# Moving one broadcast, respacing the fillers, and laying out two weight matrices anew in a fused attention and feed-forward kernel

## The chip, the cores and the metric

One core of a Trainium2 chip runs the kernel. Its engines are TensorE (PE; its weight loads are listed as PEld), VectorE (DVE), ScalarE (ACT), GpSimd (POOL) and SyncE (SP); SP and POOL also issue the DMA transfers, and a `q` behind an engine's name (SPq) marks its issuing side. The metric is the time of one execution on the device in microseconds (us), median of several runs. Lower is better.

## The reference

Sliding-window attention with a linear bias, and behind it a feed-forward block with layer norm, on 8 sequences of 576 tokens, 8 heads of 64, `d_model` 512, hidden size 2048. All inputs and the output are fp32.

```python
scores = q @ k.T / 8 - slope[h] * abs(i - j)      # only 0 <= i - j < 128
x  = softmax(scores) @ v                          # heads side by side: 512 columns
xn = (x - mean(x)) / sqrt(var(x) + 1e-6) * g_ln
out = x + relu(xn @ w_ch1) @ w_ch2                # 512 -> 2048 -> 512
```

## The kernel before

The 4608 tokens are cut into 36 blocks of 128. A block goes through attention, and blocks are then joined to ten chunks (`CHUNKS`, of 3, 2, 3 and then 4 blocks) for the feed-forward part, whose matmuls thus have 384, 256, 384 and then 512 columns.

*Attention of block i.* q and k come in on SP (`load`, L360; `load_span` for two blocks at a time, L455) or, from block 9 on, on POOL with a cast on the way (L469). Loaded fp32 is cast to fp16 on POOL, ACT or DVE (L617 for spans, L556 for block 4, L589 for v). PE turns q and k so that the head's dimension lies on the partitions: fp32 pairs against an identity for spans (L635, tasks `T0.0`, `T0.1`, ...; "the turn"), fp16 for block 4 (L682). ACT or DVE evicts the turn to `qkt` (L645, L643). For the first five blocks PE puts the bias into PSUM with a matmul (L736, `Z`); the scores go on top (L720, `S`). ACT takes the exponential (L768, `probs`), PE multiplies with v (L792, 65 columns, one of them the row's sum), and DVE divides (L809, L813), takes mean and variance (L830, L835) and writes `xs = (x - mean) * g` (L841). PE turns `xs` (L853, later by DMA), which gives `xt`. Tables for the mask and bias of later blocks (`mreg`, `mmix`, `mnew`) are made once on ACT (L433) and DVE (L441 and following).

*g.* `g_ln` is one row of 512. Task `G` (L411) broadcasts it to all partitions: an fp32 matmul of a row of ones with the row, 512 columns into a bank of PSUM, and `Gc` (L418) copies it to `g_t`, which the first `xs` reads.

*Feed-forward of chunk c.* `A{c}.{f}` (L902), for each of 16 groups f of 128 hidden columns: four matmuls, with 128 columns of W1 as the loaded weight and `xt` as the moving operand; a relu on ACT (L914) or DVE (L912) to `ht`. `B{i}` (L930), for each block of the chunk: 16 matmuls with `ht` as the loaded weight and rows of W2 moving. DVE multiplies by 1/std and adds x (L938), and SP writes the block out (L946). The last block is done in two halves of 256 columns (`cuts`).

*Weights.* W1 and W2 come in four transfers each on POOL's queue, with a cast to fp16 (`weights`, L532 and L534). They are issued behind the casts or loads listed in `W_AFTER`: the first of W1 behind block 2, the second and third behind block 3, the fourth behind block 6. A transfer of W1 brings 512 of the 2048 hidden columns, so the fourth is first read by group f = 12. A transfer of W2 brings 512 rows, on partition p the rows 512m + p, 512m + 128 + p, and so on.

*What sets the order.* `Plan` is a list scheduler that runs while the kernel is built. Every task has an engine, a cost in us, a due value `v` and what it depends on; transfers are tasks of a queue, with a cost of their own. The planner goes through simulated time, gives a free engine the ready task with the lowest `v`, and hands out four PSUM banks (`fb`) for all results but the scores. The order that comes out is emitted as the program. Each engine then runs its list strictly in order and waits on semaphores. A cost or dependency that changes can thus move tasks anywhere later in the lists.

*Fillers.* While the planned time is below 24 us (`WARM`), `keep_warm` (L966 to L968) puts small matmuls of zeros into PE's list wherever the plan has PE idle, one for each 0.11 us of gap if the gap starts before 6 us, and one for each 0.06 us later. They always run, whether PE would have waited or not.

Of the kernel before, what the change touches and what calls it, by code (L numbers as in the profile page):

```python
# [226 lines left out]
def kernel(  # L227
# [75 lines left out]
    mreg = sb("mreg", [P, 4, 2, 2 * P], FP16)  # L303
    mmix = sb("mmix", [P, 4, 2, 2 * P], FP16)
    mnew = sb("mnew", [P, 4, 2, 2 * P], FP16)
    w1sb = sb("w1sb", [P, NKB, ffn], FP16)
    w2sb = sb("w2sb", [P, NFB, d_model], FP16)

    q32 = ring("q32", 2, [P, H, D], FP32)
    k32 = ring("k32", 2, [P, H, D], FP32)  # L310
# [30 lines left out]
        return (i / CB - LEAD) * SPAN + stage  # L341

    w1r = moe_w_ch1.rearrange("(kb p) f -> p kb f", p=P)
    w2r = moe_w_ch2.rearrange("(fb p) d -> p fb d", p=P)

    def where(i):

# [69 lines left out]
        else:  # L417
            nc.scalar.activation(out=g_t[:, :], in_=src, func=AF.Copy)  # L418

    t_g = add("G", ("PE", 1.3), e_g, [d_row], av(0, 4.0), acq=("fb", "G"))  # L420
    d_g = add("Gc", {"ACT": 0.6, "DVE": 0.69}, e_gc, [t_g], av(0, 4.5), rel="G")

    t_sid = []
# [100 lines left out]
    def weights(i, casts):  # L524

        for n, at in enumerate(W_AFTER):
            if at // 3 != i:
                continue

            def emit(e, b, m=n % 4, n=n):  # L530
                if n < 4:
                    nc.gpsimd.dma_start(out=w1sb[:, :, 512 * m : 512 * m + 512], in_=w1r[:, :, 512 * m : 512 * m + 512])  # L532
                else:
                    nc.gpsimd.dma_start(out=w2sb[:, 4 * m : 4 * m + 4, :], in_=w2r[:, 4 * m : 4 * m + 4, :])  # L534
            last = [t_w[n - 1][0]] if n else []
            t_w[n] = plan.transfer(f"w{n}", "POOL", 0.8, 3.2, 0.0, emit, [casts[at % 3]] + last, av(i, -60.0))

    span_done, pv_done, qkt_part = {}, {}, {}
    qkt_done, vx_done, aggr_done, xs_done, xt_done = {}, {}, {}, {}, {}

    def attention(i):
# [62 lines left out]
        if i in span_of:  # L604
            n = span_of[i]
            if SPANS[n] == i:
                evs, casts = [[], []], {}
                for (a, x), (landed, h0, h1) in span_load[n].items():
                    r_, w_ = ((qs, qs16), (ks, ks16))[a]

                    def e_c(e, b, r_=r_, w_=w_, n=n, h0=h0, h1=h1):
                        dst = w_[n][:, h0:h1, :, :].rearrange("p h d t -> p t h d")
                        src = r_[n][:, h0:h1, :].rearrange("p h (t d) -> p t h d", t=2)
                        if e == "ACT":
                            nc.scalar.activation(out=dst, in_=src, func=AF.Copy)
                        else:
                            (nc.vector if e == "DVE" else nc.gpsimd).tensor_copy(out=dst, in_=src)  # L617
                    f = (h1 - h0) / H
                    cs = add(
                        f"cT{i}.{a}{x}", pick(f"cs{a}{x}", "POOL", POOL=0.12 + 1.26 * f, ACT=0.22 + 1.18 * f, DVE=0.1 + 0.7 * f),  # L620
                        e_c, [landed], av(i, 0.1 * a + 0.2 * x),
                    )
                    r_.reads(n, cs); w_.writes(n, cs)
                    for y in range(2) if f == 1 else (x,):
                        casts[a, y] = cs
                for x in range(2):
                    key = f"T{i}.{x}"

                    def e_t(e, b, x=x, n=n):
                        for a, w_ in ((0, qs16), (1, ks16)):  # L630
                            for hp in range(2):
                                h0 = 4 * x + 2 * hp
                                pair = w_[n][:, h0 : h0 + 2, :, :].rearrange("p h d t -> p (h d t)").bitcast(FP32)
                                c0 = (2 * a + hp) * P
                                nc.tensor.transpose(fb[b][:, c0 : c0 + P], pair, iden32[:, :])  # L635
                    tt = add(key, ("PE", 0.45), e_t, [casts[0, x], casts[1, x], d_iden32], av(i, 1.0 + 0.1 * x), acq=("fb", key))
                    qs16.reads(n, tt); ks16.reads(n, tt)
                    for blk in range(2):
                        def e_ev(e, b, x=x, blk=blk, key=key):
                            src = fb[plan.held[key][1]][:, :].bitcast(FP16).rearrange("p (a hp c) -> p a hp c", a=2, hp=2)[:, :, :, P * blk : P * blk + P]  # L640
                            dst = qkt[i + blk][:, :, 2 * x : 2 * x + 2, :]
                            if e == "DVE":
                                nc.vector.tensor_copy(out=dst, in_=src)  # L643
                            else:
                                nc.scalar.activation(out=dst, in_=src, func=AF.Copy)  # L645
                        ev = add(f"e{key}{blk}", pick(f"ev{x}{blk}", "DVE ACT", DVE=0.42, ACT=0.6), e_ev, [tt] + evs[0][len(evs[1]) :], av(i + blk, 1.2 + 0.1 * x), rel=key)
                        qkt.writes(i + blk, ev)
                        evs[blk].append(ev)
                span_done[n] = evs
# [240 lines left out]
    def mlp(c):  # L890
# [5 lines left out]
        for f in range(NFB):  # L896
            key = f"A{c}.{f}"
            vm = v0 + f * per

            def e_a(e, b, f=f):  # L900
                for kb in range(NKB):
                    nc.tensor.matmul(  # L902
                        fb[b][:, 0:n_], w1sb[:, kb, f * P : f * P + P], xt[c][:, kb, 0:n_],
                        start=(kb == 0), stop=(kb == NKB - 1),
                    )
            a = add(key, ("PE", 0.216 * nb), e_a, done + [t_w[f // 4][1]], vm, acq=("fb", key))
            xt.reads(c, a)

            def e_r(e, b, f=f, key=key):
                src = fb[plan.held[key][1]][:, 0:n_]  # L910
                if e == "DVE":
                    nc.vector.tensor_scalar(out=ht[c][:, f, 0:n_], in0=src, scalar1=0.0, scalar2=None, op0=ALU.max)  # L912
                else:
                    nc.scalar.activation(out=ht[c][:, f, 0:n_], in_=src, func=AF.Relu)  # L914
            r_ = add(f"r{c}.{f}", {"ACT": 0.17 + 0.107 * nb, "DVE": 0.16 + 0.133 * nb}, e_r, [a], vm - 4.0, rel=key)
            ht.writes(c, r_)
            relu.append(r_)
        for j in range(nb):
            i = FIRST[c] + j
            cuts = (0, d_model // 2, d_model) if i == NBLK - 1 else (0, d_model)  # L920
            for c0, c1 in zip(cuts, cuts[1:]):
                key = f"B{i}" if c1 - c0 == d_model else f"B{i}.c{c0}"
                last = None
                for f0 in range(0, NFB, 4):
                    vm = v0 + 16 * per + (4 * j + f0 / 4 + c0 / 100) * SPAN / 32

                    def e_b(e, b, j=j, f0=f0, key=key, c0=c0, c1=c1):
                        pm = fb[plan.held[key][1]]
                        for f in range(f0, f0 + 4):
                            nc.tensor.matmul(  # L930
                                pm[:, 0 : c1 - c0], ht[c][:, f, j * P : j * P + P], w2sb[:, f, c0:c1],
                                start=(f == 0), stop=(f == NFB - 1),
                            )
                    last = add(f"{key}.{f0}", ("PE", 0.864 * (c1 - c0) / d_model), e_b, relu[f0 : f0 + 4] + [t_w[4 + f0 // 4][1], last], vm, acq=("fb", key))
                    ht.reads(c, last)

                def e_o(e, b, i=i, j=j, key=key, c0=c0, c1=c1):
                    nc.vector.scalar_tensor_tensor(  # L938
                        out=ot[i][:, c0:c1], in0=fb[plan.held[key][1]][:, 0 : c1 - c0], scalar=rstd[c][:, j : j + 1],
                        in1=xb[i][:, c0:c1], op0=ALU.mult, op1=ALU.add,  # L940
                    )
                o = add(f"o{i}.{c0}", ("DVE", 0.2 + 0.55 * (c1 - c0) / d_model), e_o, [last, kept[c]], vm - 4.0, rel=key)
                ot.writes(i, o); rstd.reads(c, o); xb.reads(i, o)

                def e_d(e, b, i=i, c0=c0, c1=c1):
                    nc.sync.dma_start(out=out_flat[i * P : i * P + P, c0:c1], in_=ot[i][:, c0:c1])  # L946
                t, d = plan.transfer(f"out{i}.{c0}", "SP", 0.42, 0.8 * (c1 - c0) / d_model, 0.12, e_d, [o], vm - 4.0)
                ot.reads(i, d)
# [8 lines left out]
    for n, (at, tasks) in enumerate(cast_seq):  # L957
        before = [t_w[m][0] for m, w_at in enumerate(W_AFTER) if (w_at // 3 * 3 + 2 if w_at // 3 in span_of else w_at) < at][-1:] + (cast_seq[n - 1][1] if n and at < 27 else [])
        for t in tasks:
            t.deps += before  # L960
    for c in range(len(CHUNKS)):
        mlp(c)

    order = plan.run()

    def keep_warm(a, b):  # L966
        for _ in range(int((b - a - 0.06) / (0.11 if a < 6.0 else 0.06))):
            nc.tensor.matmul(fb[3][:, 0:P], warm_t[:, :], warm_t[:, :], start=True, stop=True)  # L968

    with tc.manual_schedule():  # L970
# [38 lines left out]
```

## Time and profile before

| | us |
|---|---|
| median of 6 runs | 320.22 (319.5 to 322.06) |
| the profiled execution | 319.98 |
| its span in the profile | 318.3 |
| PE busy | 311.5 |
| PE idle for all its waits | 3.5 |
| 592 matmuls of L930, share of the chain that ended last | 40% |
| 640 matmuls of L902, share of that chain | 38% |

Times in the profile count from the start of the span. A matmul's record is longer than its place in the queue, as matmuls overlap: one with 512 columns has a record of 379 ns, but the next starts 215 ns later. So the pace is read from start to start. The rows on loads in the timeline name the engine that issues; when a transfer lands is told by the times to landing. "<-" behind a row's idle time names what ended it.

### The profile page before, as it was taken

What the parts mean: (1) busy time and instruction counts of PE and PEld (TensorE: products, weight loads), DVE (VectorE), ACT (ScalarE), POOL (GpSimd) and SP (SyncE); (2) the same over time, 40 slices, a digit from 0 to 9 for tenths busy, and PEclk for the clock granted to TensorE, in tenths of its full rate; (3) what the DMA queues carried; (4) which work ended last, traced back from release to release, by engine and by line L of the source; (5) the groups of instructions that cost most, each with busy time, mean ns of one, the idle gap of its engine ahead of it and who ended that gap; (6) DMA issues with size and microseconds to landing.
All of it is one profiled execution on the core that took longest, in us unless ns stands there. A gap on an engine that the chain in (4) does not pass through costs nothing.

```text
span 318.3 us, 6348 instructions
## 1 busy us (share of the span) xinstructions
PE 311.5 (98%) x2540; PEld 168.3 (53%) x2540; DVE 183.9 (58%) x410; ACT 158.1 (50%) x258; POOL 101.9 (32%) x133
## 2 busy tenths in 40 slices
PE   8989999999999999999999999999999999999995
PEld 6766766545555444454444544444445444444444
DVE  2689469852789676566666666466666666011012
ACT  2587784226666861475247524752474247305600
POOL 6636685685256274543633312011000000000000
PEclk9999999999999999999999999999999999999999
DMA  8999999999999999999999999456400220011012
GB/s 196 234 185 244 208 203 175 155 193 194 144 151 182 159 154 150 191 174 155 198 176 102 102 161 165 39 67 130 119 16 19 83 85 16 16 68 66 0 60 74
DMA packets 155408, 41.45 MB, mean 130 GB/s; under 512 B 138353, under 2 KB 150897, under 8 KB 155378
## 3 DMA queue, kind: packets, MB, share of 16 engines
q0 software_dynamic: 92768, 15.34, 65.2%
q1 hardware_dynamic: 62608, 25.70, 41.7%
q8 instruction: 20, 0.33, 0.4%
q14 instruction: 10, 0.08, 0.1%
q10 hardware_dynamic: 2, 0.00, 0.0%
HBM read 36.70 MB, written 9.44 MB: 145 GB/s over the span
## 4 chain that ended last, share of the span: by engine, by line
PE 89%; SPq 4%; DMA 2%; DVE 2%; ACT 1%; issue 0%; POOL 0%; DVEq 0%
PE fb L930 40%; PE fb L902 38%; PE sc L720 5%; PE fb L792 5%; SPq L360 3%; DMA k<-in_k_dram 2%; SPq L455 2%; PE fb L853 1%; PE fb L635 0%; DVE mnew L441 0%; PE fb L968 0%; DVE xb L813 0%; ACT probs L768 0%; PE sc L736 0%; ACT ht L914 0%
## 5 line engine op out<-in xcount | busy, mean ns | idle before, releaser
L930 PE MATMUL fb<-w2sb,ht 128*128 128x512 f16 (+1 forms) x592 | 135.0, 373 | 0.0
L902 PE MATMUL fb<-xt,w1sb 128*128 128x512 f16 (+2 forms) x640 | 132.7, 358 | 0.4 <-ACT probs L768 0.4
L914 ACT ACTIVATE ht<-fb 128x512 f16<-128x512 f32 (+2 forms) x144 | 79.3, 556 | 68.4 <-PE fb L902 67.4
L768 ACT ACTIVATE probs<-sc 128x1024 f16<-128x1024 f32 (+1 forms) x72 | 67.7, 973 | 59.8 <-PE sc L720 59.5
L902 PEld LDWEIGHTS <-w1sb 128*128 128x128 f16 x640 | 59.8, 98 | 57.0 <-DMA w1sb<-in_moe_w_ch_dram 0.6
L930 PEld LDWEIGHTS <-ht 128*128 128x128 f16 x592 | 54.2, 98 | 55.0
L938 DVE SCALAR_TENSOR_TENSOR ot<-fb,rstd,xb 128x512 f32<-128x512 f32 (+1 forms) x37 | 27.2, 735 | 56.2 <-PE fb L930 55.5
L469 POOL DMA_DIRECT2D vx<-in_v_dram x34 | 28.9, 853 | 63.6 <-PE fb L792 58.1
L775 DVE TENSOR_TENSOR probs<-probs,mreg 128x1024 f16<-128x1024 f16 (+1 forms) x48 | 30.7, 651 | 20.3 <-ACT probs L768 20.0
L469 POOL DMA_DIRECT2D qk<-in_q_dram x30 | 25.3, 845 | 23.3 <-DMA qkt<-qk 12.5
L792 PEld LDWEIGHTS <-probs 128*128 128x128 f16 x544 | 24.8, 98 | 14.1 <-ACT probs L768 0.6
L813 DVE TENSOR_TENSOR xb<-fb,rec 128x256 f16<-128x256 f32 x72 | 30.2, 423 | 2.1
L469 POOL DMA_DIRECT2D qk<-in_k_dram x30 | 25.3, 844 | 14.7 <-DMA vx<-in_v_dram 5.1
L841 DVE SCALAR_TENSOR_TENSOR xs<-xb,mv,g_t 128x512 f16<-128x512 f16 x36 | 27.7, 768 | 0.9
L792 PE MATMUL fb<-vx,probs 128*128 128x65 f16 x544 | 27.8, 193 | 0.0
L830 DVE BATCH_NORM_STATS2 st<-xb 128x6 f32<-128x512 f16 x36 | 24.8, 692 | 1.0
L809 DVE RECIPROCAL rec<-fb 128x4 f32<-128x4 f32 x72 | 12.6, 177 | 19.3 <-PE fb L792 19.1
L720 PEld LDWEIGHTS <-qkt 64*128 64x128 f16 x544 | 15.3, 94 | 11.8 <-issue 10.6
L720 PE MATMUL sc<-qkt 64*128 64x128 f16 x288 | 19.8, 216 | 0.0
L720 PE MATMUL sc<-qkt,qkt 64*128 64x128 f16 x256 | 18.4, 219 | 0.0
L912 DVE TENSOR_SCALAR ht<-fb 128x512 f16<-128x512 f32 (+2 forms) x16 | 9.9, 616 | 10.6 <-PE fb L902 9.3
L968 PE MATMUL fb<-warm_t 128*128 128x128 f16 x90 | 9.3, 258 | 1.1 <-DVE warm_t L372 1.1
(59 smaller groups left out, 111.6 us busy)
## 6 DMA issues: line engine op xcount, KB each, us to landing
out_dram<-ot SPq DMA_DIRECT2D x35, 256.0 KB, 3.7
vx<-in_v_dram POOLq DMA_DIRECT2D x28, 128.0 KB, 9.5
qk<-in_q_dram POOLq DMA_DIRECT2D x24, 128.0 KB, 10.9
qk<-in_k_dram POOLq DMA_DIRECT2D x24, 128.0 KB, 11.0
w1sb<-in_moe_w_ch_dram POOLq DMA_DIRECT2D x4, 512.0 KB, 9.2
w2sb<-in_moe_w_ch_dram POOLq DMA_DIRECT2D x4, 512.0 KB, 11.7
qs<-in_q_dram SPq DMA_DIRECT2D x4, 256.0 KB, 4.4
ks<-in_k_dram SPq DMA_DIRECT2D x4, 256.0 KB, 4.7
```

Source lines behind the costliest of these rows:

```text
L469: nc.gpsimd.dma_start(out=dst(p0, n), in_=src[b, :, s0 : s0 + n, :].rearrange("h p d -> p h d"))
L720: nc.tensor.matmul(scs[half][:, g, c0 : c0 + P], kt[rows, 1, hp, :], qkt[i][rows, 0, hp, :], start=not bias, stop=True, skip_group_check=True,
L768: nc.scalar.activation(out=o, in_=n_, func=AF.Exp, scale=inv_sqrt_d)
L775: en.tensor_tensor(out=pv, in0=pv, in1=mask[:, 2 * half : 2 * half + 2, :, lo:], op=ALU.mult)
L792: nc.tensor.matmul(pp[:, hh * (D + 1) : hh * (D + 1) + D + 1], probs[i][:, bank, slot, side * P : side * P + P], vx[i - 1 + side][:, h, 0 ...
L813: nc.vector.tensor_tensor(out=xb[i][:, 256 * half : 256 * half + 256].rearrange("p (h d) -> p h d", d=D), in0=pp[:, :, 0:D], in1=rec[2 * i ...
L830: nc.vector.bn_stats(out=st[i][:, :], in_=xb[i][:, :])
L841: nc.vector.scalar_tensor_tensor(out=xs[i][:, :], in0=xb[i][:, :], scalar=mv[c][:, j, 0:1], in1=g_t[:, :], op0=ALU.subtract, op1=ALU.mult,)
L902: nc.tensor.matmul(fb[b][:, 0:n_], w1sb[:, kb, f * P : f * P + P], xt[c][:, kb, 0:n_], start=(kb == 0), stop=(kb == NKB - 1),)
L914: nc.scalar.activation(out=ht[c][:, f, 0:n_], in_=src, func=AF.Relu)
L930: nc.tensor.matmul(pm[:, 0 : c1 - c0], ht[c][:, f, j * P : j * P + P], w2sb[:, f, c0:c1], start=(f == 0), stop=(f == NFB - 1),)
L938: nc.vector.scalar_tensor_tensor(out=ot[i][:, c0:c1], in0=fb[plan.held[key][1]][:, 0 : c1 - c0], scalar=rstd[c][:, j : j + 1], in1=xb[i][: ...
```

## The change

Five edits. Task `G` gets half its planned cost and a dependency on the first turn (`first_turn`), so that it stands behind it. Fillers count by 0.11 us up to a planned time of 8.5 us instead of 6. W1 becomes four tiles, one for a transfer, and W2 as well. A transfer of W2 now brings, on partition p, the four rows 512m + 4p to 512m + 4p + 3, which lie side by side in HBM (8 KB); for the rows to fit, the weight of group f = 4m + j is every fourth column of W1's tile m, from column j on (`w1f`). W2's planned transfer is 2.7 us instead of 3.2. The last block is cut into 384 and 128 columns.

```diff
@@ -303,8 +303,8 @@
-    w1sb = sb("w1sb", [P, NKB, ffn], FP16)
-    w2sb = sb("w2sb", [P, NFB, d_model], FP16)
+    w1sb = [sb(f"w1sb{m}", [P, NKB, CH], FP16) for m in range(CB)]
+    w2sb = [sb(f"w2sb{m}", [P, CB, d_model], FP16) for m in range(CB)]
@@ -341,7 +341,8 @@
-    w2r = moe_w_ch2.rearrange("(fb p) d -> p fb d", p=P)
+    w2r = moe_w_ch2.rearrange("(m p j) d -> p m (j d)", p=P, j=CB)
+    w1f = [t[:, :, :].rearrange("p kb (c j) -> p kb j c", j=CB) for t in w1sb]
@@ -417,7 +418,7 @@
-    t_g = add("G", ("PE", 1.3), e_g, [d_row], av(0, 4.0), acq=("fb", "G"))
+    t_g = add("G", ("PE", 0.65), e_g, [d_row], av(0, 4.0), acq=("fb", "G"))
@@ -529,13 +530,13 @@
                 if n < 4:
-                    nc.gpsimd.dma_start(out=w1sb[:, :, 512 * m : 512 * m + 512], in_=w1r[:, :, 512 * m : 512 * m + 512])
+                    nc.gpsimd.dma_start(out=w1sb[m][:, :, :], in_=w1r[:, :, 512 * m : 512 * m + 512])
                 else:
-                    nc.gpsimd.dma_start(out=w2sb[:, 4 * m : 4 * m + 4, :], in_=w2r[:, 4 * m : 4 * m + 4, :])
+                    nc.gpsimd.dma_start(out=w2sb[m][:, :, :].rearrange("p j d -> p (j d)"), in_=w2r[:, m, :])
             last = [t_w[n - 1][0]] if n else []
-            t_w[n] = plan.transfer(f"w{n}", "POOL", 0.8, 3.2, 0.0, emit, [casts[at % 3]] + last, av(i, -60.0))
+            t_w[n] = plan.transfer(f"w{n}", "POOL", 0.8, 3.2 if n < 4 else 2.7, 0.0, emit, [casts[at % 3]] + last, av(i, -60.0))
-    span_done, pv_done, qkt_part = {}, {}, {}
+    span_done, pv_done, qkt_part, first_turn = {}, {}, {}, []
@@ -634,6 +635,7 @@
                     tt = add(key, ("PE", 0.45), e_t, [casts[0, x], casts[1, x], d_iden32], av(i, 1.0 + 0.1 * x), acq=("fb", key))
+                    first_turn.append(tt)
@@ -900,7 +902,7 @@
-                        fb[b][:, 0:n_], w1sb[:, kb, f * P : f * P + P], xt[c][:, kb, 0:n_],
+                        fb[b][:, 0:n_], w1f[f // CB][:, kb, f % CB, :], xt[c][:, kb, 0:n_],
@@ -917,7 +919,7 @@
-            cuts = (0, d_model // 2, d_model) if i == NBLK - 1 else (0, d_model)
+            cuts = (0, 3 * P, d_model) if i == NBLK - 1 else (0, d_model)
@@ -928,7 +930,7 @@
-                                pm[:, 0 : c1 - c0], ht[c][:, f, j * P : j * P + P], w2sb[:, f, c0:c1],
+                                pm[:, 0 : c1 - c0], ht[c][:, f, j * P : j * P + P], w2sb[f // CB][:, f % CB, c0:c1],
@@ -958,13 +960,14 @@
+    t_g.deps.append(first_turn[0])
     for c in range(len(CHUNKS)):
         mlp(c)
...
-        for _ in range(int((b - a - 0.06) / (0.11 if a < 6.0 else 0.06))):
+        for _ in range(int((b - a - 0.06) / (0.11 if a < 8.5 else 0.06))):
             nc.tensor.matmul(fb[3][:, 0:P], warm_t[:, :], warm_t[:, :], start=True, stop=True)
```

In the changed kernel line numbers are higher by one to three: L902 is L904, L930 is L932, L968 is L971.

## The prediction

> **What bounds the kernel now.** I read the page's busy times first, then who TensorE (PE) waited for, then the PE timeline of the first 45 us, then the last 10 us.
>
> ```profile
> PE 311.5 (98%) x2540; PEld 168.3 (53%) x2540; DVE 183.9 (58%) x410; ACT 158.1 (50%) x258; POOL 101.9 (32%) x133
> ...
> engine line waited for: us in total, times, longest us
> PE fb L968 <- DVE warm_t L372: 1.1, 1, 1.1
> PE fb L682 <- POOL qk L556: 1.0, 1, 1.0
> PE fb L853 <- ACT rstd L882: 0.4, 1, 0.4
> PE fb L902 <- ACT probs L768: 0.4, 1, 0.4
> ```
>
> PE is never idle but for 3.5 us in all. A change can gain only by taking work off PE (the fillers of L968 are the only useless work), by removing one of these waits, or at the two ends. So the question for each part is whether what it saves reaches the end of PE's queue or runs into one of these waits.
>
> The start (start, length, engine, line):
>
> ```profile
> 3.07 1.06 PE L736 MATMUL sc<-dist_t,sid 128*128 128x128 f16 x8
> 4.06 2.07 PE L411 MATMUL fb<-ot,ot 1*128 1x512 f32 x2
> 6.07 0.71 PE L968 MATMUL fb<-warm_t 128*128 128x128 f16 x5
> 6.57 0.64 PE L635 MATMUL fb<-iden,qs 128*128 128x128 f32 x2
> 7.00 0.63 PE L635 MATMUL fb<-iden,ks 128*128 128x128 f32 x2
> 7.43 1.59 PE L968 MATMUL fb<-warm_t 128*128 128x128 f16 x13
> 8.95 0.29 PE L720 MATMUL sc<-qkt 64*128 64x128 f16 x4
> ```
>
> g's broadcast (L411) holds PE for 2.01 us, from 4.06 to 6.07. The first turn (L635) comes at 6.57, though POOL had its last cast at 5.50 (4.74 plus 0.76). Then 13 fillers hold the first scores from 7.43 to 8.95, 117 ns each, while ACT had evicted the turn by 8.27.
>
> Further on, the weights:
>
> ```profile
> 40.47 0.61 PE L902 MATMUL fb<-xt,w1sb 128*128 128x256 f16 x4
> 41.44 2.12 PE L902 MATMUL fb<-xt,w1sb 128*128 128x384 f16 x12 [0.35 <-ACT probs L768]
> ...
> 41.43 1.74 PEld L902 LDWEIGHTS <-w1sb 128*128 128x128 f16 x12 [0.63 <-DMA w1sb<-in_moe_w_ch_dram]
> ...
> 29.20 0.95 POOL L532 DMA_DIRECT2D w1sb<-in_moe_w_ch_dram  x1
> ...
> DMA to landing us min/median/max: 9.0/10.6/12.2
> ```
>
> The PE row blames ACT for the wait before 41.44, but its weight load names the W1 transfer. The fourth W1 transfer is issued at 29.20 and takes the longest of its window, 12.2 us: it lands at 41.4. Chunk 0's thirteenth column group (f = 12) is the first to read it. This is the point that I build on: whatever PE does before, it goes on at 41.4. The four matmuls from 40.47 end their pass after 4 x 109 ns, at 40.91, so 0.52 us are lost here.
>
> **The change, part by part.** The base is the profiled execution, 319.98 us; its span is 318.28 and 1.7 lie outside.
>
> *g behind the first turn, and the fillers.* In the changed order 18 fillers follow the eight L736, then the turn, one filler, g, the first scores. The fillers before had 105 ns each (19 from 1.07 to 3.07), so the turn starts at 4.06 + 18 x 0.107 = 5.99, 0.58 us sooner, and ends its pass at 6.85. With a clock as slow as before, g then runs from 6.96 to 8.97, and the first scores start where they did (8.95). With a fast one (the fillers at 9.17 have 60 ns each) g takes half, and they start near 7.95, 1.0 us sooner. Neither is seen at the end: block 4's turn (L682) waits 0.97 us at 22.64 for POOL's cast of k, which POOL starts at 21.97 after 3.83 idle us behind a DMA, and these loads are issued by SP, which none of this touches. A PE that is 1 us ahead waits 1 us longer there. Price 0, bounds 0 and, if that cover and the next were gone, -1.0.
>
> The Trainium skill ("TensorE: Matmul & The Clock Gate", Part 1) says that the cold phase is a free-running activity window of about 3.4 us whose phase differs from run to run, and warns against fitting a cold count. It speaks against counting fillers by 0.11 us up to 8.5. By its rule the two clocks above may change places between runs; by the row (cold up to 8.95) they don't; the sum is the same, as both end in the wait at 22.64.
>
> *What the planner makes of it up to 41.4.* I counted both orders up to the first matmul that reads the fourth W1 transfer. Scores, P.V, transposes, bias and chunk 0's matmuls are equal in number; the fillers are 99 for 90; and chunk 1's first matmuls (128x256) are 28 for 36. Eight of these, two column groups, are moved behind the wait. From 22.64 the kernel before took 18.3 us to get to 40.91. Changed, this span loses 8 x 0.109 = 0.87 and 6 of 18 fillers (0.37), and gains eight scores and eight P.V that stood ahead of the cast (0.28 + 0.24): PE arrives at about 40.2. On ACT four table exponentials (411 ns) and two probs (1020 ns) now stand ahead of the second relu of chunk 0, which keeps the bank for PE some 0.4 us longer: 40.6. It is ahead of 41.4 and waits 0.8 instead of 0.52. From there PE owes 0.87 us more than before: +0.87. If the transfer landed 0.8 us sooner, it would be 0; if PE came 1 us later than I count, +1.1. I take +0.87, because the POOL rows that lead to the issue at 29.20 (a cast behind the landing of qs at 27.81) stand in the same order.
>
> *W2 in 8 KB runs.* Now 2048 packets of 1024 B at 98 ns, on 16 engines 12.5 us. 512 packets of 4096 B cost 174 ns each at the rate of the output's 2048 B packets (87 ns) and, at worst, counted by bytes read at the rate of the 16 KB instruction packets (1080 ns), 540 ns: 5.6 to 17.3 us in all. No one waits for the gain. For the loss: the four land at 44.73, 47.36, 49.87 and 54.95, and by the sum over the changed order are first read near 46.9, 49.1, 51.6 and 57.6. At the bad end each is 1.2 us longer and PE loses about 2. I take 0: bounds 0 and +2.
>
> *W1's columns with a step of four.* Every one of 640 weight loads of L902 now reads each fourth element. No row has such a load.
>
> ```profile
> 13.93 0.42 PE L792 MATMUL fb<-vx,probs 128*128 128x65 f16 x8
> 14.18 0.60 PE L736 MATMUL sc<-dist_t,sid 128*128 128x256 f16 x4
> ...
> L902 PEld LDWEIGHTS <-w1sb 128*128 128x128 f16 x640 | 59.8, 98 | 57.0 <-DMA w1sb<-in_moe_w_ch_dram 0.6 <-DVE xt L861 0.3
> ...
> L635 PEld LDWEIGHTS fb<-iden,ks 128*128 128x128 f32 x16 | 2.2, 152 | 0.0
> ```
>
> Eight L792 take 0.25 us, each with a full load: a contiguous load fits into 31 ns. The slowest load of the trace, fp32, is 152 ns. What hides it are the matmuls: 215 ns at 512 columns (448), 162 at 384 (128), 109 at 256 (64). At 31 ns the price is 0; at 152 only the 64 show it, 64 x 43 ns = 2.8 us. I take 0, as it is fp16 and nearer to L792's row; bounds 0 and +2.8.
>
> The skill says two things. "TensorE: Matmul & The Clock Gate" (Weight-path perf modes) lets the fast load take a column step up to 1024 elements: by it, 0. "SBUF — State Buffer" (Specifications) has 16-byte lines that need two hits for full speed, which speaks against steps in general; a step of 8 bytes has just two: again 0.
>
> *The tail.*
>
> ```profile
> 313.84 0.48 DVE L938 SCALAR_TENSOR_TENSOR ot<-fb,rstd,xb 128x256 f32<-128x256 f32 x1 [0.18 <-PE fb L930]
> 315.09 0.48 DVE L938 SCALAR_TENSOR_TENSOR ot<-fb,rstd,xb 128x256 f32<-128x256 f32 x1 [0.77 <-PE fb L930]
> ```
>
> 512 columns take 0.75 on DVE, 256 take 0.48, so 128 about 0.35: -0.13. The last transfer halves: eight packets an engine of 512 B (29 to 33 ns) for 1024 B (47 ns): -0.13. PE: 16 x 162 + 16 x 60 (a filler's pace, with its load) for 32 x 109: +0.06. The 384-column part is issued about 0.7 us ahead of the last and has landed. Sum -0.2, bounds -0.35 and 0.
>
> Sum: 319.98 + 0.87 - 0.2 = 320.65. The median is 0.24 above the profiled run, which would make 320.9; I say **320.8**.
>
> **Rivals.** (1) *The waits go*: the fourth W1 transfer lands sooner, and PE runs on. Then before's 0.52, its 0.4 at L853, 0.34 at the turn at 49.1 and the tail come off, +0.15 for work moved behind 22.64: 318.7, and 317.8 if the start's gain passes too; 318.5. For it: only 0.8 us of wait is in the way. Against: no part touches that transfer's issue, and its packets stay 1024 B. (2) *Strided loads show*, slower: 320.65 + 2.8 = 323.4, from the point where a load takes longer than 109 ns. For it: the load's duration has never been this pattern; against: the room of 162 and 215 ns. (3) *PE comes late to 41.4 or to W2*: ACT's exponentials keep the banks, or W2 lands late; 1 to 2 us, 322.2. Against: 0.8 and 1.7 us of room. (4) *The early part does nothing*, as with the slow clock above: that is in the forecast.
>
> **How the numbers follow.** About 0.5% (1.6 us) is what a measurement of this kernel tells from no change: 318.6 to 321.8. Forecast 0.50 (within 0.42, slower 0.07, faster 0.01; own range 319.8 to 321.8); rival 1 0.17 (faster 0.11); rival 2 0.18 (slower 0.17); rival 3 0.15 (slower 0.14). Faster 0.12, same 0.50, slower 0.38. Range 319.0 to 324.0: below lies most of rival 1, above the ends of 2 and 3, together under 0.2.
>
> **What would show it.** The turn at 6.0 instead of 6.57, and the cast's wait at 22.6 longer; a wait of 0.6 to 1.0 us ended by the W1 transfer at 41.4 (none there means rival 1, PE later than 41.4 rival 3); L902 at 109, 162 and 215 ns start to start (more at 256 means rival 2); the last DVE instruction of 0.35 us. The forecast is wrong if that W1 transfer moves.

## The result, and the profile after

| | before | changed |
|---|---|---|
| median of the runs, us | 320.19 (319.04 to 323.83, 70 runs) | 322.58 (321.29 to 324.32, 33 runs) |
| ratio | | 1.0072 [1.0059, 1.0085] |
| span of the profiled execution | 318.3 | 320.3 |
| granted clock of that execution | 1.000 | 1.000 |

The changed kernel is 0.72% slower. The two spans differ by 2.0 us, and both have a granted clock of 1.000, so the traces can be compared piece by piece. (The clock records of a trace begin with PE's first moment of full clock, at 8.98 us before and at 4.31 in the change; the slower stretch ahead of it is counted as 1.00.) First the page's busy row, and below it the waits of TensorE (columns: us in total, times, longest):

```profile
PE 311.0 (97%) x2549; PEld 176.5 (55%) x2549; DVE 185.2 (58%) x413; ACT 157.4 (49%) x256; POOL 101.4 (32%) x132
```

```profile
engine line waited for: us in total, times, longest us
PE fb L904 <- DMA w1sb<-in_moe_w_ch_dram: 3.0, 3, 1.7
PE fb L971 <- DVE warm_t L373: 1.1, 1, 1.1
PE sc L722 <- ACT qkt L647: 0.9, 1, 0.9
PE fb L636 <- DVE xb L815: 0.5, 1, 0.5
```

PE is busy 0.5 us less and yet ends later. It waits for W1 three times. The wait of 1.0 us for the cast of k (L682 before, L684 now) is gone. Where the lead comes from is seen in PE's timeline of the start (start, length, engine, line):

```profile
3.92 1.36 PE L971 MATMUL fb<-warm_t 128*128 128x128 f16 x18
5.12 0.39 PE L636 MATMUL fb<-iden,qs 128*128 128x128 f32 x2
5.55 0.44 PE L636 MATMUL fb<-iden,ks 128*128 128x128 f32 x2
5.83 0.22 PE L971 MATMUL fb<-warm_t 128*128 128x128 f16 x1
5.97 1.12 PE L412 MATMUL fb<-ot,ot 1*128 1x512 f32 x2
7.03 0.28 PE L722 MATMUL sc<-qkt 64*128 64x128 f16 x4
```

The 18 fillers take 1.2 us, 67 ns each, where 19 before took 105 each. g's broadcast takes 1.06 us from start to start instead of 2.01, and the first scores start at 7.03 instead of 8.95. So PE is 1.9 us ahead in these two profiles. This lead is not the change's alone. e1 (below) has before's list here, with g at 4.06, and its rows are:

```profile
4.06 1.12 PE L412 MATMUL fb<-ot,ot 1*128 1x512 f32 x2
...
5.85 0.89 PE L969 MATMUL fb<-warm_t 128*128 128x128 f16 x13
6.70 0.29 PE L721 MATMUL sc<-qkt 64*128 64x128 f16 x4
```

There g takes 1.06 us too, 13 fillers take 65 ns each, and the first scores start at 6.70. What differs is the first moment of full clock, 4.02 in e1, and it differs between executions of the same list. Further on in the change:

```profile
20.65 0.61 PE L684 MATMUL fb<-iden,qk 128*128 128x128 f16 x8
...
29.18 2.79 PE L904 MATMUL fb<-xt,w1sb 128*128 128x384 f16 x16 [0.71 <-DMA w1sb<-in_moe_w_ch_dram]
...
32.91 4.54 PE L904 MATMUL fb<-xt,w1sb 128*128 128x384 f16 x32 [0.65 <-DMA w1sb<-in_moe_w_ch_dram]
...
41.96 2.14 PE L904 MATMUL fb<-xt,w1sb 128*128 128x384 f16 x12 [1.65 <-DMA w1sb<-in_moe_w_ch_dram]
...
49.51 0.41 PE L636 MATMUL fb<-iden,qs 128*128 128x128 f32 x2 [0.51 <-DVE xb L815]
```

Block 4's turn (L684) comes at 20.65 with no wait. Before, its second half waited until 22.64:

```profile
22.64 0.40 PE L682 MATMUL fb<-iden,qk 128*128 128x128 f16 x4 [0.97 <-POOL qk L556]
```

Then the whole lead is waited away at the second, third and fourth transfer of W1, and the first matmul that reads the fourth starts at 41.96 instead of 41.44. From here on there is only one more wait that counts, at the turn of 49.51. Before, it was shorter:

```profile
49.11 0.44 PE L635 MATMUL fb<-iden,qs 128*128 128x128 f32 x2 [0.19 <-DVE xb L813]
```

Two cuts of the span make the comparison simple: the first matmul on the fourth W1 transfer, and the start of PE's last matmul.

| stretch | before | changed | difference |
|---|---|---|---|
| start to the first read of the fourth W1 transfer | 41.44 | 41.96 | +0.52 |
| from there to the last matmul's start | 273.35 | 275.07 | +1.72 |
| from there to the end of the span | 3.49 | 3.25 | -0.24 |

The sum is +2.00. The middle stretch can be trusted to some hundredths: four profiles with before's PE order in it gave 273.34 to 273.40, and two with the changed kernel's order and loads gave 275.07 each.

### The profile page after: what moved, and what is told of

It is laid out like the page before. It is cut to its first block, busy times and chain, and to the rows that moved or that the text cites. A ratio compares the mean times of both kernels' runs of the same rounds, so it can differ in the third digit from the quotient of the medians.

```text
span 320.3 us, 6367 instructions
## 1 busy us (share of the span) xinstructions
PE 311.0 (97%) x2549; PEld 176.5 (55%) x2549; DVE 185.2 (58%) x413; ACT 157.4 (49%) x256; POOL 101.4 (32%) x132
## 4 chain that ended last, share of the span: by engine, by line
PE 86%; DMA 7%; SPq 5%; issue 1%; DVE 0%; POOL 0%; POOLq 0%; DVEq 0%
PE fb L932 39%; PE fb L904 36%; PE sc L722 5%; PE fb L794 4%; DMA w1sb<-in_moe_w_ch_dram 4%; SPq L361 3%; DMA qs<-in_q_dram 3%; SPq L456 2%; PE fb L855 1%; PE fb L636 0%; POOL qs L618 0%; DVE ot L940 0%; DVE xb L815 0%; DVE rec L811 0%; POOLq L618 0%
## 5 line engine op out<-in xcount | busy, mean ns | idle before, releaser
L904 PE MATMUL fb<-xt,w1sb 128*128 128x512 f16 (+2 forms) x640 | 133.9, 359 | 3.0 <-DMA w1sb<-in_moe_w_ch_dram 3.0
L932 PE MATMUL fb<-w2sb,ht 128*128 128x512 f16 (+2 forms) x592 | 134.2, 373 | 0.0
L916 ACT ACTIVATE ht<-fb 128x512 f16<-128x512 f32 (+2 forms) x140 | 77.8, 559 | 67.6 <-PE fb L904 66.2
L904 PEld LDWEIGHTS <-w1sb 128*128 128x128 f16 x640 | 68.8, 114 | 51.2 <-DMA w1sb<-in_moe_w_ch_dram 3.8
L932 PEld LDWEIGHTS <-ht 128*128 128x128 f16 x592 | 53.9, 98 | 56.6
L940 DVE SCALAR_TENSOR_TENSOR ot<-fb,rstd,xb 128x512 f32<-128x512 f32 (+2 forms) x37 | 27.2, 735 | 59.6 <-PE fb L932 58.7
L843 DVE SCALAR_TENSOR_TENSOR xs<-xb,mv,g_t 128x512 f16<-128x512 f16 x36 | 27.0, 750 | 1.0
L914 DVE TENSOR_SCALAR ht<-fb 128x512 f16<-128x512 f32 (+2 forms) x20 | 12.1, 603 | 7.6 <-ACT probs L770 3.8
L971 PE MATMUL fb<-warm_t 128*128 128x128 f16 x99 | 8.9, 240 | 1.1 <-DVE warm_t L373 1.1
```

The costliest lines, as they stand in the source:

```text
L843: nc.vector.scalar_tensor_tensor(out=xs[i][:, :], in0=xb[i][:, :], scalar=mv[c][:, j, 0:1], in1=g_t[:, :], op0=ALU.subtract, op1=ALU.mult,)
L904: nc.tensor.matmul(fb[b][:, 0:n_], w1f[f // CB][:, kb, f % CB, :], xt[c][:, kb, 0:n_], start=(kb == 0), stop=(kb == NKB - 1),)
L932: nc.tensor.matmul(pm[:, 0 : c1 - c0], ht[c][:, f, j * P : j * P + P], w2sb[f // CB][:, f % CB, c0:c1], start=(f == 0), stop=(f == NFB - 1),)
L940: nc.vector.scalar_tensor_tensor(out=ot[i][:, c0:c1], in0=fb[plan.held[key][1]][:, 0 : c1 - c0], scalar=rstd[c][:, j : j + 1], in1=xb[i][: ...
```

## The experiments

Twelve kernels were run, each against the kernel before on the same chip, all but one in five rounds (12 runs). "Ahead" counts chunk 1's matmuls of 256 columns that PE does before it first reads the fourth W1 transfer (36 before, 28 in the change). "First read" and "rest" are the first two stretches above. "At full clock" is the median of those runs whose mean granted clock was 0.998 or more; why it is there is told under the last four. For the changed kernel the record has the clocks of 34 runs, one more than its median. A ratio is to the runs of before that were taken beside that kernel, with medians of 320.19 (changed), 320.83 (e1 to e4), 320.55 (e5 to e8) and 320.88 (f1 to f4). "First read" and "rest" come from one profile each. Those of e6, e7, f3 and f4 hold a stretch of 3.4 us at half clock, ahead of the first read in e6, e7 and f4 and in the rest of f3.

| kernel | median us | ratio to before | ahead | first read | rest | at full clock (runs) |
|---|---|---|---|---|---|---|
| before | 320.19 | | 36 | 41.44 | 273.35 | 320.19 (68 of 104) |
| changed | 322.58 | 1.0072 | 28 | 41.96 | 275.07 | 321.90 (16 of 34) |
| e1_layout | 321.47 | 1.0021 [0.999, 1.0051] | 36 | 42.26 | 273.68 | 320.83 (6) |
| e2_front | 323.09 | 1.0069 [1.0038, 1.0101] | 28 | 41.90 | 274.88 | 322.00 (4) |
| e3_after_w1cost36 | 321.93 | 1.0033 [1.0007, 1.0059] | 36 | 42.39 | 274.59 | 321.72 (8) |
| e4_after_w1cost45 | 320.47 | 1.0002 [0.9972, 1.0032] | 44 | 42.28 | 273.78 | 320.41 (10) |
| e5_fillers | 320.02 | 0.9995 [0.9974, 1.0016] | 36 | 41.34 | 273.34 | 319.94 (11) |
| e6_before_w1cost44 | 321.57 | 1.0019 [0.9995, 1.0043] | 44 | 43.72 | 274.25 | 321.35 (11) |
| e7_step16 | 321.75 | 1.0028 [1.0004, 1.0053] | 36 | 43.44 | 274.65 | 321.74 (9) |
| e8_after_issue_sooner | 321.24 | 1.0016 [0.9994, 1.0038] | 24 | 39.27 | 276.30 | 321.09 (11) |
| f1_before_issue_sooner | 320.25 | 0.9957 [0.9933, 0.9981] | 36 | 42.00 | 273.34 | 320.25 (12) |
| f2_before_fillers_cut | 320.04 | 0.9983 [0.996, 1.0007] | 36 | 42.08 | 273.40 | 319.88 (10) |
| f3_before_sooner_fillers_cut | 320.24 | 0.9986 [0.9959, 1.0013] | 36 | 42.28 | 274.99 | 319.94 (7) |
| f4_after_sooner_same_list | 322.77 | 1.0061 [1.0034, 1.0088] | 28 | 40.81 | 275.07 | 321.67 (4) |

### Which half costs the time

**e1_layout**: the kernel before with the W1 and W2 part of the change alone (tiles, `w1f`, `w2r`); the planned transfer of W2 stays at 3.2, and the order of every engine is before's.

> The kernel before with W1 in four tiles, its columns read with a step of four, and W2 in 8 KB runs; the planned costs stay, so that each engine's list stands as before. Theory (the time follows from when the fourth W1 transfer lands and from the work that stands behind that wait): 36 matmuls of 128x256 are still ahead of the wait, so 320.2 to 320.6, a wait of about 0.5 us at 41.4, and 256-column matmuls of L902 still 109 ns apart. Rival (the strided loads, or W2's larger packets, cost the 2.3 us): 322 to 323, and a longer distance from start to start somewhere in L902, or a wait for W2.

**e2_front**: the kernel before with the g part and the fillers alone.

```diff
-    t_g = add("G", ("PE", 1.3), e_g, [d_row], av(0, 4.0), acq=("fb", "G"))
+    t_g = add("G", ("PE", 0.65), e_g, [d_row], av(0, 4.0), acq=("fb", "G"))
+                    first_turn.append(tt)
+    t_g.deps.append(first_turn[0])
-        for _ in range(int((b - a - 0.06) / (0.11 if a < 6.0 else 0.06))):
+        for _ in range(int((b - a - 0.06) / (0.11 if a < 8.5 else 0.06))):
```

> The kernel before with g behind the first turn, its planned cost of 0.65 and the fillers by 0.11 us up to 8.5; weights and tail as before. Theory: 28 instead of 36 matmuls of 128x256 ahead of the fourth W1 transfer, PE waits there 1.2 to 1.8 us, and 0.87 us of work is owed behind it: 321.4 to 322.4, most of the whole change. Rival (loads or W2): 320.2, nothing of the loss is here.

The front costs as much as the whole change: 1.0069 beside 1.0072. By its ratio the layout alone can't be told from nothing; its six runs at full clock are 0.6 us above before's, and in its profile the first read is 0.8 us later (the fourth transfer landed at 42.22) and the rest 0.33 us longer. The rest of e2 is 1.53 us longer than before's, with before's loads. 0.87 is the time of the eight matmuls that now stand behind the wait, at 109 ns each (the debt), and the other 0.67 is wait. This is the waits view of e2:

```profile
PE fb L903 <- DMA w1sb<-in_moe_w_ch_dram: 2.9, 1, 2.9
...
PE fb L931 <- DVE xb L814: 0.6, 1, 0.6
```

In e2, PE first waits 2.9 us at the fourth W1 transfer with nothing ahead of it to do, and soon after, at 50.3, for VectorE. Before, the gap at the turn near 49 us was 0.35 us over the plain pace; in e2 the two gaps there are 0.76 and 0.26, together 0.67 more.

### Is the debt the cause

**e3_after_w1cost36** and **e4_after_w1cost45**: the changed kernel with only the planned time of the fourth W1 transfer longer, so that the planner puts 36 or 44 matmuls ahead of its reader.

```diff
-            t_w[n] = plan.transfer(f"w{n}", "POOL", 0.8, 3.2 if n < 4 else 2.7, ...
+            t_w[n] = plan.transfer(f"w{n}", "POOL", 0.8, 3.6 if n == 3 else 3.2 if n < 4 else 2.7, ...
```

> The changed kernel with the planned cost of the fourth W1 transfer at 3.6 us instead of 3.2, nothing else: the planner then puts 36 matmuls of 128x256 ahead of the wait, as before the change. Theory: the wait of 1.65 us falls by 0.87 to about 0.8, and the time by as much: 322.58 to about 321.7. Rival (the loss is in the loads): 322.6 as the changed kernel.

> The same with 4.5 us: 44 matmuls of 128x256 ahead of the wait. Theory: the wait is all but gone (1.65 less 1.74), the time falls by about 1.6 us to 320.9 to 321.0, near the kernel before. Rival (the loss is in the loads): 322.6; if only the landing counts and not what stands behind it: 322.6 too.

With 28, 36 and 44 ahead the ratio goes 1.0072, 1.0033, 1.0002: each step of 0.27% of work (0.87 of 320 us) gave 0.3 to 0.4%. At full clock, though, the first step gives only 0.2 us (321.90 to 321.72) and the second 1.3. e3's rest shows why: it is 0.48 us shorter than the changed kernel's, not 0.87, since PE has a new gap of 0.75 us at 60.8 us, where a P.V matmul waits for VectorE. So the debt is a cause, but the order that comes with another count brings waits of its own.

**e6_before_w1cost44**: the same lever on the kernel before (planned transfer 4.0 for 3.2).

> The kernel before with the planned cost of the fourth W1 transfer at 4.0 us instead of 3.2, nothing else: 44 instead of 36 matmuls of 128x256 stand ahead of the wait. Theory: the wait of 0.5 to 0.9 us at the fourth W1 transfer goes, and the time falls by that, to 319.4 to 319.7 (ratio 0.998). Rival (what is moved ahead only moves the wait to another transfer, W2's or the next block's): 320.2.

This was a miss. PE no longer waits for W1, which was the aim, and the time did not fall:

```profile
PE fb L682 <- POOL qk L556: 1.9, 1, 1.9
...
PE fb L902 <- DVE xb L813: 0.7, 1, 0.7
PE fb L930 <- DVE ht L912: 0.5, 1, 0.5
PE fb L792 <- DVE xb L813: 0.4, 1, 0.4
```

The three lower waits lie between 60 and 69 us, and before has none of them. So in the order that came with the work moved ahead, PE waits for VectorE some 20 us later: the rest is 0.90 us longer than before's with 0.87 us less work in it. In this profile PE also came late to its old mark: the fourth transfer landed at 41.58, and PE first read it at 43.72. Ahead of that stood 0.87 us more work, the wait of 1.9 us for the cast of k, and behind this wait a stretch at half clock. In these windows the first figure is the length, then come busy PE, PEld, DVE, ACT and POOL, then the clock:

```profile
20.00:23.40 3.40, 1.64 (x33) 1.21 (x29) 2.50 (x7) 2.58 (x5) 0.50 (x1) 1.00 1.22 240
23.40:26.80 3.40, 3.23 (x27) 2.74 (x27) 1.01 (x3) 2.03 (x5) 3.11 (x5) 0.50 1.21 223
26.80:30.00 3.20, 3.19 (x59) 2.56 (x58) 2.19 (x6) 2.62 (x5) 1.63 (x2) 1.00 1.19 250
```

So e6's first read can't be compared with the others. Its time can: the other eleven runs are at full clock, with a median of 321.35.

### The parts that were priced at nothing

**e5_fillers**: the kernel before with the 8.5 alone.

```diff
-        for _ in range(int((b - a - 0.06) / (0.11 if a < 6.0 else 0.06))):
+        for _ in range(int((b - a - 0.06) / (0.11 if a < 8.5 else 0.06))):
```

> The kernel before with the fillers by 0.11 us up to 8.5 and nothing else: 82 fillers instead of 90, every other list as before. Theory (PE's lead at the start is waited away, at the cast of k or at the fourth W1 transfer): 320.2, within 0.2%, though the first scores start some 0.8 us sooner. Rival (the start counts): 319.4.

Nothing, as expected (0.9995): what PE gains at the start (the first scores at 8.32 instead of 8.95) it waits away, 1.8 us of it at the fourth W1 transfer in this profile. e1 says the same with more: its first scores came 2.25 us sooner than before's, and its first read of the fourth transfer, at 42.26, no sooner.

**e7_step16**: the kernel before with W1 in tiles of its own and loads of every sixteenth column.

```diff
+    w1f = [t[:, :, :].rearrange("p kb c -> p (kb c)").rearrange("p (c j) -> p j c", j=4 * CB) for t in w1sb]
-                        fb[b][:, 0:n_], w1sb[:, kb, f * P : f * P + P], xt[c][:, kb, 0:n_],
+                        fb[b][:, 0:n_], w1f[f // CB][:, CB * kb + f % CB, :], xt[c][:, kb, 0:n_],
```

> The kernel before with W1 in four tiles and its weights read with a step of 16 elements (32 bytes); order as before. It multiplies with W1's elements in a scrambled order, so its output is not the reference's. Theory (weight loads hide behind matmuls of 109 ns and more as long as they are shorter): the load's record grows beyond 98 ns, the 215 and 162 ns stay, and the time is within 0.5% of before. Rival (a load of a longer step shows): more than 109 ns at 256 columns, or more than 215 at 512, and then a loss of 5 us and more.

The load's row, in the changed kernel (step 4), and then in e7 (step 16); the columns are busy us and mean ns of one:

```profile
L904 PEld LDWEIGHTS <-w1sb 128*128 128x128 f16 x640 | 68.8, 114 | 51.2 <-DMA w1sb<-in_moe_w_ch_dram 3.8
```

```profile
L903 PEld LDWEIGHTS <-w1sb 128*128 128x128 f16 x640 | 87.9, 146 | 32.1 <-DVE xt L862 0.3
```

98 ns before, 114 with a step of four, 146 with a step of sixteen. From start to start most matmuls keep their pace: the medians for 256, 384 and 512 columns are 109, 162 and 216 ns before, 109, 163 and 216 in the change, 109, 162 and 216 in e7. Most loads are thus hidden even where their record, 146 ns, is longer than the matmul's 109. A remainder shows in the rest. e1 has before's order and step-4 loads, and its rest is 0.33 us longer; e7's, with before's order too, is 1.30 us longer. Nearly all of it lies in a few of the 412 distances at 512 columns: 11 of 242 to 245 ns in e1 and 30 of 246 to 276 ns in e7, while before has none above 227. At full clock e7 is 1.5 us slower than before.

### When the fourth transfer lands

**e8_after_issue_sooner**: the changed kernel with that transfer issued three casts sooner. The planner knows of it and makes another order (24 ahead).

```diff
-    W_AFTER = [8, 10, 11, 20, 21, 22, 23, 28]
+    W_AFTER = [8, 10, 11, 17, 21, 22, 23, 28]
```

> The changed kernel with the fourth W1 transfer issued behind block 5's loads instead of block 6's, ahead of the cast of qs on POOL. Theory: it lands some 2 to 3 us sooner, PE's wait of 1.65 us falls to 0.5 or less, and the time to 321.0 to 321.5. Rival (all transfers share one bandwidth): what now lands later, qs, ks or v of the next blocks, is waited for in its place, and the time stays at 322.6.

It lands at 39.23, 2.7 us sooner. The ratio is 1.0016 for the change's 1.0072, and at full clock the kernel is 0.8 us faster than the change, though it starts with one column group less ahead and its rest is 1.23 us longer. So in the two profiles PE keeps 1.5 of the 2.7 us; the rest goes to work that now stands behind the landing. The next runs tried to have it without another order. **f1** and **f4** move the same issue in GpSimd's finished list, from behind the cast of q of block 5 to just ahead of it, in the kernel before and in the changed kernel; PE's list stays.

```diff
+    w4 = next(x for x in order if x[0].name == "w3.i")
+    order.remove(w4)
+    order.insert(next(n for n, x in enumerate(order) if x[0].name == "cT5.00"), w4)
```

> The kernel before with one change: on GpSimd's list the issue of the fourth W1 transfer stands ahead of the fp32-to-fp16 cast of q of block 5 instead of behind it; every other list is as it was. Theory (the issue waits behind that cast, so the transfer lands late and PE stands for it): issue near 25 to 26 us instead of 29.2, landing 39.2 to 39.6 instead of 41.4, PE's wait of 0.5 us at the thirteenth column group gone; but PE can keep only what no later wait takes back, so 319.2 to 319.9 us, ratio 0.996 to 0.999. Rival A (q, k and v of the next blocks share the DMA engines with it, land later, and PE stands for them between 40 and 55 us): wait for W1 gone, but ratio 1.000 or above. Rival B (the landing is set by how busy the DMA engines are, not by the issue): landing stays at 41 or later, ratio 1.000.

> The changed kernel with only the issue of the fourth W1 transfer moved ahead of the cast of q of block 5 on GpSimd's list; PE's list is the changed kernel's, with two column groups of chunk 1 behind that transfer's wait as there. Theory: landing 39.2 to 39.8 instead of 41.9, PE's wait of 1.7 us there shrinks to at most 0.3, PE keeps most of it: 321.0 to 321.6, ratio to the kernel before 1.002 to 1.005. Rival (what is gained there is waited away again between 42 and 60 us): 322.3 to 322.8, ratio 1.006 to 1.009.

f1's theory fell and its rival B held. GpSimd's timeline of f1 (start, length), and then that of the changed kernel:

```profile
24.89 1.76 POOL L469 DMA_DIRECT2D vx<-in_v_dram  x2
26.64 0.92 POOL L532 DMA_DIRECT2D w1sb<-in_moe_w_ch_dram  x1
27.71 1.33 POOL L617 CAST qs<-qs 128x1024 f16<-128x1024 f32 x1 [0.16 <-DMA qs<-in_q_dram]
28.95 0.89 POOL L469 DMA_DIRECT2D vx<-in_v_dram  x1
```

```profile
24.15 1.76 POOL L470 DMA_DIRECT2D vx<-in_v_dram  x2
26.95 1.35 POOL L618 CAST qs<-qs 128x1024 f16<-128x1024 f32 x1 [1.03 <-DMA qs<-in_q_dram]
28.20 0.95 POOL L533 DMA_DIRECT2D w1sb<-in_moe_w_ch_dram  x1
29.14 0.89 POOL L470 DMA_DIRECT2D vx<-in_v_dram  x1
```

f1 issues W1 at 26.64, the change at 28.20, and both land it at 41.9 (41.95 and 41.91). The landings of GpSimd's queue say why. Its third W1 transfer, two of v, the fourth W1 and the next v land at 32.5, 36.0, 39.0, 41.95 and 42.8 in f1, and at 32.9, 36.0, 39.1, 41.9 and 42.8 in the change. They come one after the other in order of issue, 2.8 to 3.5 us apart (the last after 0.85), and there is always one outstanding. What counts here is the place in this queue, not the moment of the issue. In e8 the transfer stood one v further ahead (24.42 v, 25.30 W1), and it landed at 39.23, just where the second v lands elsewhere. In f4 it was issued at 24.79 and landed at 40.76; there the whole queue ran ahead (the third W1 landed at 31.1, the two of v at 34.2 and 37.6), and the distances are the same. f4's median, 322.77, is the changed kernel's and lies in the range of f4's rival, but not by its mechanism: in f4's profile PE kept the sooner landing (the rest is 275.07, as in the change, and the span 1.1 us shorter). That profile is the fastest of f4's 12 runs; where the transfer landed in the others is not known.

**f2** is the kernel before with the fillers and the cut of the last block (`cuts = (0, 3 * P, d_model)`), **f3** adds f1's sooner issue.

> The kernel before with two parts of the change that leave all of PE's order up to the last block alone: fillers by 0.11 us up to a planned 8.5 us, and the last block cut into 384 and 128 columns. Theory: the fillers give 0, the cut gives 0.24 us as the tail of the changed kernel's profile shows (3.25 us behind the last matmul's start instead of 3.49): ratio 0.999 to 1.000, tail 3.2 to 3.3. Rival (the tail's gain is chance): tail 3.45 to 3.5.

> The kernel before with the sooner issue of the fourth W1 transfer, the fillers and the cut of the two runs ahead of it together. If the parts add: 0.2 us less than the sooner issue alone, so 318.9 to 319.7, ratio 0.995 to 0.998: faster than both kernels. If the sooner issue only moves the wait: 320.0, ratio 0.999 to 1.000.

The tail is 3.26 in f2 and 3.25 in f3, as in the change, so the cut's 0.24 us holds; f2's rest gives 0.05 of it back (273.40 for 273.35). With the time alone, 0.9983 [0.996, 1.0007], it can't be told from nothing. f3's 320.24 is what was expected if the sooner issue gains nothing (320.0).

f1's ratio of 0.9957 with an unmoved landing needs another reason, and the granted clock gives it. The executions of all kernels fall in two groups, with a mean clock of 0.998 and more or of 0.995 and less. Before's medians in these are 320.19 (68 runs) and 322.12 (36 runs). All 12 runs of f1 happened to be in the first group, where its median of 320.25 is before's. f3's profile shows what the lower clock is. Its windows, in the form of e6's:

```profile
40.00:43.00 3.00, 0.81 (x6) 0.46 (x6) 1.02 (x2) 1.31 (x2) 0.90 (x1) 1.00 1.54 195
43.00:46.00 3.00, 3.00 (x23) 1.73 (x22) 0.65 (x2) 0.98 (x2) 3.00 (x5) 0.54 1.25 207
46.00:49.00 3.00, 3.00 (x35) 2.42 (x32) 1.92 (x5) 2.15 (x4) 3.00 (x4) 0.89 1.38 198
```

From 43.22 to 46.63, just after PE's wait of 2.2 us for W1, the clock is at half. f3's rest is 274.99, 1.59 longer than f2's, which has the same list of PE. One such stretch in 320 us gives a mean clock of 0.995. The change had 18 of its 34 runs in the lower group, before 36 of 104.

What brings such a stretch on can be read from the clock records of the 14 profiles. Four of them have one in the middle: f4 from 7.89, e6 from 23.40, e7 from 24.02 and f3 from 43.22. Each is 3.41 us long, and each begins 1, 4, 4 and 10 times 3.41 us after that profile's first moment of full clock. In the 3.41 us ahead of it PE was idle for 0.83 (f4, and g's one-row matmul took 1.05 more), 1.76, 1.69 and 2.19 us. Of all other spans of 3.41 us, counted in the same way, none has more than 1.70 us of idle PE (e4, which kept its clock). So by these profiles a wait is followed by half the clock when about 1.7 us of it fall into one such span. In e2's profile the wait of 2.9 us was parted into 1.36 and 1.54, and the clock stayed; 8 of e2's 12 runs are in the lower group. The changed kernel's wait of 1.65 us had 1.55 in one span, near the limit. That this is why its runs fall into the lower group more often is argued, not shown: no profile of it holds such a stretch.

At full clock the change is 1.7 us slower than before (321.90 and 320.19), which is the 2.0 of the profiles within what a landing varies; the rest of the 2.4 between the medians is its larger share of runs at a lower clock. At full clock no kernel tried is faster than before by more than about 0.3 us.

## Why the prediction came out as it did

The forecast was 320.8, with a range of its own from 319.8 to 321.8. What came, 322.58, lies above it, and inside 319.0 to 324.0 only because the rivals had widened that range. By the prediction's own bound of 321.8 the change is told from no change: slower, to which it gave 0.38. Of the 1.8 us that it fell short, 1.33 lie between the two profiles (+2.00 for +0.67): 0.85 behind the landing, 0.52 the landing itself, -0.04 the tail. 0.36 lie between profile and median (0.60 for 0.24), as more of the runs hold a stretch at half clock, and 0.1 is rounding.

*Where PE goes on.* "Whatever PE does before, it goes on at 41.4" was right in kind, and with it price 0 for the start: in the change PE was 2 us ahead and went on at 41.96. That this transfer should move was named as a sign of being wrong. It moved by 0.52, but kernels with before's order up to there landed it anywhere between 41.29 (e5) and 42.85 (e7), so this half microsecond can't be laid to the change. The turn was said to start at 6.0 and the first scores at 7.95 or 8.95; they started at 5.12 and 7.03, since the full clock began at 4.31 and not at 8.98. The prediction set two readings of the clock side by side: by the rule that it cites the slow and the fast clock may change places between runs, by before's row they do not. The runs agree with the rule: with g at 4 us the full clock began at 3.73 to 4.08 in three profiles (f1, e1, f2) and at 8.98 to 10.37 in five (before, f3, e5, e6, e7). The lead was to be waited away at the cast of k at 22.6; it was waited away at three W1 transfers. Where it is lost varies between kernels with nearly the same lists up to there: f2 issued its first W1 transfer at 15.00, ahead of SP's last load of k at 15.43, which then landed at 21.56, and PE waited 2.1 us for the cast of k and 1.9 for W1; f1 issued it at 16.14, behind that load (15.29, landed at 19.04), and PE waited 3.1 us for W1 and 1.2 for ACT. They first read the fourth transfer at 42.08 and 42.00.

*The planner's +0.87.* This was the right place and the right mechanism: two column groups moved behind the fourth transfer, and PE owes them from there. It is the term that was mis-sized. The stretch behind the landing became 1.72 us longer, not 0.87:

| | us |
|---|---|
| eight matmuls of 256 columns, as predicted | 0.87 |
| the gap at the turn of 49 us, 0.67 instead of 0.35 over the pace | 0.32 |
| step-4 loads (e1's rest) | 0.33 |
| a gap behind four P.V matmuls at 66.53: the next starts 0.26 later instead of 0.13 | 0.13 |
| the last block's cut (f2's rest) | 0.05 |
| not found | 0.02 |

PE was said to arrive at 40.6 and lose 0.8; it ended its pass at about 40.1 and lost 1.8 (1.65 by the row, as records end later than the pass). The 0.4 us for ACT's exponentials did not come. The step that failed is that the debt was counted as if all behind the wait ran as before. There PE waits for VectorE to empty what it writes to next (the releaser at 49.51 is `xb`), and in the new order it met VectorE at another point. e2 shows this without the loads (0.87 + 0.67 for its 1.53).

*Loads with a step.* Price 0 was nearly right: 0.33 us in e1's rest, within the bounds of 0 and 2.8. It shows at 11 of the 512-column distances, not at 256 columns, where the prediction looked for it. The Trainium skill's page "SBUF — State Buffer" (Specifications) asks for two hits in a line of 16 bytes, which a step of 8 bytes still has, and says that each crossing to a new line pays a penalty, without a figure. The trace has the load at 114 ns for 98, so by the measurement a step of four fp16 elements is not quite free.

*W2 as 8 KB runs.* Price 0 was right. The four landed at 45.18, 47.70, 50.46 and 55.14, each 0.2 to 0.6 us later than before, and were first read at 47.50, 50.42, 53.02 and 59.18, with no wait. GpSimd's issue of one became shorter, 0.53 to 0.58 us for 0.74 to 0.94, which nobody waits for.

*The tail.* -0.2 was predicted. The tail became 0.24 shorter and the stretch ahead of it 0.05 longer by the cut (f2), so -0.19 came. The timeline's last row on VectorE has the 0.35 that was worked out:

```profile
317.29 0.35 DVE L940 SCALAR_TENSOR_TENSOR ot<-fb,rstd,xb 128x128 f32<-128x128 f32 x1 [0.22 <-PE fb L932]
```

*The rivals.* Rival 3, PE late, has the nearest time (322.2), but that is luck: PE came early to the transfer and no W2 was waited for. Rival 1 fell, as the landing did not come sooner. Rival 2 fell: its 2.8 us were 64 loads that show at 256 columns, and even in e7, with a load longer than the matmul, the median there stayed at 109 ns; the 1.30 us that e7's loads did cost lie at 512 columns.

## What to carry to other kernels

Find the transfer at which the critical engine goes on again, and ask of a change not what it saves ahead of it but what the order puts behind it: a lead ends in the wait, a debt is paid in full, and the waits of the later order come on top. When a transfer in a full queue is late, move it past other transfers; an earlier issue in the same place brought nothing here (f1). Before a ratio of half a per cent is explained, look at how the granted clocks of the two sets of runs are spread.

## What was not expected of the hardware

- Loads of weights with a column step of 4 and 16 fp16 elements have records of 114 and 146 ns (98 contiguous). Most stayed hidden behind matmuls that follow each other every 109 ns; a few distances at 512 columns grew to 242 to 276 ns, 0.33 us in all with a step of 4 and 1.30 with 16.
- PE's first moment of full clock varies between executions of one list. With g's one-row fp32 matmul at 4 us it came at 3.73 to 4.08 in three profiles and at 8.98 to 10.37 in five; with 18 fillers in its place it came at 4.31 to 6.23 in all six. The profile's clock column reads 1.00 ahead of it, where fillers take 105 to 117 ns for some 60 to 67 after it.
- Transfers on GpSimd's queue landed in order of issue whatever their moment of issue: 26.64 and 28.20 both gave 41.9.
- A stretch of 3.41 us at half the granted clock costs 1.6 us (f3), and four of four began a whole number of 3.41 us after the first moment of full clock, behind a span in which PE stood idle or at a one-row matmul for 1.7 us or more. Of before's runs, the group with the lower mean clock was 1.9 us slower.
